# Issuing loads and stores from ScalarE's queue in a fused threshold-attention and MLP kernel

## The chip, the cores and the metric

The kernel runs on one core of one Trainium2 chip. The metric is the device time of one execution in microseconds (us). The core has TensorE (PE; its weight loads are shown apart as PEld), VectorE (DVE), ScalarE (ACT), GpSimd (POOL) and SyncE (SP). Each works through its own list of instructions in program order, and they wait for each other through semaphores. A DMA is started by an instruction in the list of one of these engines. "SPq" and "ACTq" in the profile are such issuing instructions on SyncE and ScalarE; the profile doesn't count them as busy time, but the queue they stand in is taken for as long as they last.

## The reference

All numbers are float32. `tau` is 0.02.

```python
# q, k, v: (8 batches, 8 heads, 576 rows, 64)
scores = 0.125 * (q @ k.T)                              # 576 x 576 for each head
scores = where(scores >= max(scores, axis=-1) - tau, scores, -1e9)
attn = exp(scores - max(scores, axis=-1))
attn = attn / (sum(attn, axis=-1) + 1e-9)
x = (attn @ v)                                          # regrouped: 4608 tokens x 512
h = maximum(x @ w_in, 0.0)                              # w_in: 512 x 2048
out = (h * h) @ w_out                                   # w_out: 2048 x 512, out: 4608 x 512
```

## The kernel before

**Work.** Attention is cut into *visits*. A visit is a pair of heads of one batch; there are 4 pairs per batch. The first batch is visited in two halves (visits 0 to 3 and 4 to 7), every other pair once (visits 8 to 35). A visit consists of *steps*: a step is a block of 128 query rows of both heads, and the last step of a full visit holds the remaining 64 rows of both. So a full visit has five steps.

A step does this. `scores` (L199) multiplies queries by keys into two PSUM tiles `s0`, `s1`, which exist once, and VectorE takes the row maxima (L204). `exponents` (L213, L215) runs on ScalarE. `threshold` (L227) on VectorE compares the scores with the threshold, multiplies and sums; after it the score tiles are free for the next step. `divide` (L237, L239) on GpSimd scales by the sum.

The attention weights must then be turned (keys onto partitions) for the product with the values, `mix` (L318). In the first visits PE turns them (L257) and ScalarE copies them out. From visit 11 on (`by_dma`) VectorE turns 32 x 32 blocks into the buffer `turned` (L288, two slots), and 48 DMAs per visit, 16 at a time, place the blocks in `wT` (L299, L306 in `place_blocks`). `mix` follows its step with a lag of four steps, and ScalarE copies its result into the ring `xT` (L332 to L347).

When 256 tokens are complete, the MLP for this *chunk* is put on a list of *pieces*: 16 pieces for the first product (L367, with ReLU on ScalarE, L377, and the square on GpSimd, L378), and then the second product. For chunks 0 and 1 that is `mlp_out` (L398); later ones use 14 pieces, `product` (L430), with sums and differences on VectorE (L441 to L457) that build the output rows `osb`.

**Order.** The program writes out the order for every engine by hand. One loop goes over the steps. In each step four calls of `fill(quarter)` take pieces from the list and put them between the parts of attention, so that PE always has MLP work beside attention. What follows a piece on other engines (`then`) is put down after the next piece, in `after`. The pieces left when attention is over run at the end.

**Loads and stores.** `load_qk(n)` (L161, L163) loads the query and key rows of visit `n` with 10 DMAs; `load_v(n)` (L171, L173) the values with 4. For full visits the rows of the next visit are loaded at the start of the second step, into one buffer each (`ql`, `kl`), which VectorE turns into `qT` and `kT` in `prep` (L178) at the end of the last step. The values go into two buffers in turn, and their loads are written at the end of the last step. `store_rows` (L411) stores 128 or 256 rows of output. All of these stand in SyncE's list, with the loads of the MLP weights (L122, early visits) and the placements: 1764 issues in all. Only visit 0's six key loads stand in ScalarE's.

Of the kernel before, what the change touches and what calls it, by code (L numbers as in the profile page):

```python
# [2 lines left out]

# [16 lines left out]
def kernel(  # L20
# [10 lines left out]
    nc = tc.nc  # L31
    B, H, S, D = q.shape
    d_model, d_ff = moe_w_in.shape
    n_tokens = out.shape[0]
    P = 128
    HP = H // 2
    NPAIR = B * HP
    NBLK = S // P
# [40 lines left out]
    at = RAW * 2 * WP  # L79
# [18 lines left out]
    osb = const.tile([P, 2, d_model], FP32, name="osb")  # L98
# [48 lines left out]
    def rows_of(n):  # L147
        return rows_in[n % 2 if n <= 2 * HP else 0]

    def load_qk(n):  # L150


        b, h = divmod(visits[n][0], HP)
        h *= 2
        for x, t in zip(rows_of(n), (q, k)):
            queue = nc.scalar if n == 0 and t is k else nc.sync
            for m in range(4):
                src = t[b, h + m // 2, :, (m % 2) * 32:(m % 2) * 32 + 32].rearrange("(c p) d -> p c d", p=32)
                last = REST // 32 if t is k and m >= 2 else 0
                to = x[m * 32:(m + 1) * 32, :, :]  # L160
                queue.dma_start(out=to[:, last:, :], in_=src[:, 0:S // 32 - last, :])  # L161
                if last:
                    queue.dma_start(out=to[:, 0:last, :], in_=src[:, S // 32 - last:, :])  # L163

    def load_v(n):
        b, h = divmod(visits[n][0], HP)
        h *= 2
        t = vs[n % 2]
        for u in range(2):
            at = u * (NBLK + 1)  # L170
            nc.sync.dma_start(out=t[:, at:at + NBLK, :],  # L171
                              in_=v[b, h + u, 0:NBLK * P, :].rearrange("(c p) d -> p c d", p=P))
            nc.sync.dma_start(out=t[u * D:(u + 1) * D, at + NBLK, :], in_=v[b, h + u, NBLK * P:S, :])  # L173

    def prep(n):

        for to, rows in zip((qT, kT), rows_of(n)):
            nc.vector.transpose(to, rows.rearrange("p c d -> p (c d)"))  # L178
        if NBLK in visits[n][1]:
            for u in range(2):  # L180
                rows = slice(u * D, (u + 1) * D)
                nc.gpsimd.tensor_copy(out=qmid[rows, u * D:(u + 1) * D], in_=qT[rows, NBLK * P:S])
# [127 lines left out]
    def mix(n, cols):  # L310
# [12 lines left out]
        def to(first, count):  # L323
            at = (lo + first) % RING
            assert at + count <= RING
            return xT[:, pr, at:at + count]
# [16 lines left out]
        else:  # L343
            fit = nq if whole else RING - lo % RING
            for x0, x1 in ((0, fit), (fit, nq)):
                if x0 < x1:
                    nc.scalar.copy(to(x0, x1 - x0), ps[:, x0:x1])  # L347

    ring3 = [6, 5, 7]
# [56 lines left out]

    def store_rows(j, t0, t1):
        lo = j * TCH  # L410
        nc.sync.dma_start(out=out[lo + t0 * P:lo + t1 * P, :].rearrange("(t p) d -> p t d", p=P), in_=osb[:, t0:t1, :])  # L411

# [2 lines left out]
    def product(j, x, half):  # L417

        if x == 0 and half == 0:
            a, c, b = ring3[2], ring3[0], ring3[1]  # L420
            used["abc"] = a, b, c
            ring3[:] = [b, a, c]
        a, b, c = (bank[y][:, 0:HD] for y in used["abc"])
        p = PRODUCTS[x]
        g0, g1 = g[:, 0:HF, :], g[:, HF:, :]
        left, slot, to = {
            "1": (g0[:, :, 0:P], Q00, a), "5": (gsum[0], FT1, c), "6": (gsum[1], FT2, b), "2": (g1[:, :, 0:P], Q10, a),
            "7": (gsum[0], FT3, b), "4": (g1[:, :, P:], FT4, a), "3": (gsum[1], Q11, c)}[p]
        for f in range(half * HF // 2, (half + 1) * HF // 2):
            nc.tensor.matmul(to, left[:, f, :], wo[:, slot, f, :], start=(f == 0), stop=(f == HF - 1))  # L430
        if not half:
            return []

        def halves(fn):
            for lo in (0, HF // 2):
                fn(slice(lo, lo + HF // 2))

        def then():
            add, sub, tt, u = ALU.add, ALU.subtract, nc.vector.tensor_tensor, u_sum
            if p == "1":  # L440
                nc.scalar.copy(p1s, a)  # L441
            elif p == "5":
                halves(lambda f: tt(out=gsum[0][:, f, :], in0=g0[:, f, 0:P], in1=g0[:, f, P:], op=sub))  # L443
            elif p == "6":
                tt(out=u, in0=b, in1=p1s, op=add)  # L445
                tt(out=osb[:, 0, HD:], in0=c, in1=u, op=add)
                halves(lambda f: tt(out=gsum[1][:, f, :], in0=g1[:, f, 0:P], in1=gsum[1][:, f, :], op=sub))
            elif p == "2":
                tt(out=osb[:, 0, 0:HD], in0=a, in1=p1s, op=add)  # L449
            elif p == "7":  # L450
                tt(out=u, in0=b, in1=u, op=add)
                tt(out=osb[:, 1, HD:], in0=c, in1=u, op=add)
            elif p == "4":
                tt(out=osb[:, 1, 0:HD], in0=u, in1=a, op=sub)
                store_rows(j, 1, 2)
            else:
                tt(out=osb[:, 0, HD:], in0=c, in1=osb[:, 0, HD:], op=add)  # L457
                store_rows(j, 0, 1)
        return [then]


# [32 lines left out]
    chunk_at, j = {}, 0  # L494
# [6 lines left out]
    state = {"us": 0.0, "left": 0.0, "step": 0, "rounded": 0, "then": []}  # L501
# [27 lines left out]
        return best  # L529

    def after():
        for fn in state["then"]:
            fn()
        state["then"] = []

    def fill(us):
        state["left"] += us
        while waiting and state["left"] >= PIECE_US / 2 and waiting[0][0] <= state["rounded"]:
            _, fn, *what = waiting.popleft()
            state["left"] -= PIECE_US  # L540
            if fn is mlp_out or what[0] <= PLAIN and what[1] == 0:
                after()
            then = fn(*what)
            after()
            state["then"] = then

# [26 lines left out]
    for s in range(END + 1):  # L573
        state["step"] = s
        on = s < NST
        now = []
        if on:
            n, i = steps[s]
            at = visits[n][1].index(i)
            last = at == len(visits[n][1]) - 1  # L580
            now = list(range(done, done + pieces[s]))
            done += pieces[s]
            more = n + 1 < len(visits)
            short = n < 2 * HP
            if short and at == 0 and 0 < n + 1 < 2 * HP:
                load_qk(n + 2)
            elif not short and at == 1 and more:
                load_qk(n + 1)
            if now:
                round_weights(now[0], 0)  # L590
            scores(s)
        old = steps[s - 2] if 2 <= s < NST + 2 and not by_dma(steps[s - 2][0]) else None
        at_once = now or old or early()
        lay = on and last and more and not by_dma(n)
        if old:
            turn(*old, 0)
            turn(*old, 1)
        if on:
            if at_once:
                exponents(n, i)  # L600
            if lay:
                prep(n + 1)
            elif now:
                round_weights(now[0], 1)
                round_weights(now[0], 2)
        if s in mixes and not old:
            mix(*mixes[s])
            for j in chunk_at.get(s, ()):
                add_chunk(j)
        if 0 < s <= NST and by_dma(steps[s - 1][0]):  # L610
            m, x = steps[s - 1]
            turn_blocks(m, x)
            if x % 2 or x == NBLK:
                place_blocks(m, x // 2)
        quarter = rate(s) / 4 if s < END else 1e9
        fill(quarter)
        if s in mixes and old:
            mix(*mixes[s])
            for j in chunk_at.get(s, ()):
                add_chunk(j)  # L620
        if old:
            turn(*old, 2)
        if on:
            if not at_once:
                exponents(n, i)
            threshold(n, i)
            if last and more and not lay:
                prep(n + 1)
            if lay and now:
                round_weights(now[0], 1)  # L630
                round_weights(now[0], 2)
        fill(quarter)
        if on:
            divide(n, i)
        fill(quarter)
        fill(quarter)
        if on:
            if now:
                end_rounding(now[0])
            for p in now[1:]:  # L640
                for stage in range(3):
                    round_weights(p, stage)
                end_rounding(p)
            if at == 0 and 0 < n <= 2 * HP:
                load_v(n)
            elif last and more and n >= 2 * HP:
                load_v(n + 1)
    after()
    assert not waiting


# [30 lines left out]
```

## Time and profile before

The median of three runs is 1451.44 us (1451.18 to 1452.18).

| what | value |
|---|---|
| profiled execution | 1450.02 us |
| its span, first to last instruction | 1448.2 us |
| mean granted TensorE clock | 0.992 |
| PE busy | 1387.1 us, 96% of the span |
| PE weight loads busy | 1058.0 us, 73% |
| VectorE busy | 904.5 us, 62% |
| GpSimd busy | 623.9 us, 43% |
| ScalarE busy | 423.1 us, 29% |
| DMA, mean of 16 engines, 300 to 1290 us | 0.51 |
| chain that ended last, share of the span | PE 65%, SPq 20%, DVE 6% |

The span is that of the slowest core, here the only one. Busy time is the time in which the engine executes instructions; the chain follows the last instruction back, at each step to what released it or to the instruction before it on its engine. Three parts can be told apart: the start and the visits that PE turns (to about 260 us, with the MLP weights being loaded and rounded beside them), the visits turned by DMA with MLP pieces between (about 260 to 1290 us), and the last chunks alone (about 1290 us to the end).

### The profile page before, as it was taken

The page shows a single profiled execution, that of the slowest core. Times are in us where ns is not written, and L with a number is a line of the kernel's source. Part 1 is how long each engine was busy: PE and PEld are TensorE (multiplying, and loading weights), DVE is VectorE, ACT ScalarE, POOL GpSimd, SP SyncE. Part 2 cuts the span into 40 slices and gives each one's busy share as a digit, 9 for nine tenths or more (in the row PEclk, how much of TensorE's full clock was granted, in tenths as well). Part 3 has the DMA queues.
Part 4 walks back from the last instruction along what each step waited for, and adds up shares of the span by engine and source line. Part 5 has one row for each costly group of instructions (what it writes and reads, how often), then busy time and mean ns, then how long its engine had stood idle before and what let it go on. Part 6 is the DMA issues. An engine that isn't in the chain of part 4 may idle for free.

```text
span 1448.2 us, 22131 instructions
## 1 busy us (share of the span) xinstructions
PE 1387.1 (96%) x7412; PEld 1058.0 (73%) x7412; DVE 904.5 (62%) x1930; ACT 423.1 (29%) x904; POOL 623.9 (43%) x794
## 2 busy tenths in 40 slices
PE   5898888999999999999999999999999999999998
PEld 3676555747787777777777777777777777788887
DVE  5899886568766676666675767666667666631011
ACT  3666554223222322222322222222222222210100
POOL 3588765425343444343343435343434352422321
PEclk9899999999999999999999999999999999999999
DMA  7564442345445545545455454555554445440000
GB/s 149 119 140 109 112 112 52 55 84 96 85 96 91 109 85 96 88 92 88 97 96 105 84 96 85 95 89 100 95 101 84 89 90 91 90 81 19 5 15 15
DMA packets 532528, 125.94 MB, mean 87 GB/s; under 512 B 523712, under 2 KB 523712, under 8 KB 532416
## 3 DMA queue, kind: packets, MB, share of 16 engines
q1 hardware_dynamic: 529984, 124.24, 44.7%
q8 instruction: 60, 0.98, 0.3%
q10 hardware_dynamic: 2400, 0.30, 0.2%
q14 instruction: 52, 0.43, 0.1%
q0 software_dynamic: 32, 0.00, 0.0%
HBM read 48.63 MB, written 9.44 MB: 40 GB/s over the span
## 4 chain that ended last, share of the span: by engine, by line
PE 65%; SPq 20%; DVE 6%; issue 3%; DMA 2%; ACT 2%; POOL 1%; DVEq 0%; ACTq 0%; POOLq 0%
PE bank L367 26%; PE bank L430 16%; SPq L299 12%; PE s L199 9%; PE bank L318 8%; SPq L306 5%; PE bank L398 3%; SPq L161 3%; DVE st L204 2%; PE bank L257 1%; SPq L163 1%; DVE w L227 1%; DVE turned L288 1%; DMA vs<-in_v_dram 1%; DVE turned L138 1%
## 5 line engine op out<-in xcount | busy, mean ns | idle before, releaser
L367 PE MATMUL bank<-xT,w_in_sb 128*128 128x256 f32 x2304 | 519.8, 382 | 3.5 <-POOL w_in_sb L144 2.4
L367 PEld LDWEIGHTS bank<-xT,w_in_sb 128*128 128x128 f32 x2304 | 431.6, 190 | 84.2 <-issue 21.3
L204 DVE TENSOR_REDUCE st<-s 128x1 f32<-128x576 f32 x288 | 206.7, 753 | 296.9 <-PE s L199 296.9
L378 POOL TENSOR_TENSOR g<-g 128x512 f32<-128x512 f32 x144 | 149.8, 1042 | 232.2 <-ACT g L377 209.4
L239 POOL TENSOR_SCALAR w<-w,st 128x576 f32<-128x576 f32 x269 | 236.4, 888 | 31.2 <-DVE st L230 25.2
L227 DVE SCALAR_TENSOR_TENSOR w<-s,st,w 128x576 f32<-128x576 f32 x269 | 207.3, 803 | 52.2 <-ACT w L215 51.9
L430 PE MATMUL bank<-wo,gsum 128*128 128x256 f32 x1024 | 234.2, 382 | 2.9 <-DVE u_sum L445 1.6
L430 PEld LDWEIGHTS bank<-wo,gsum 128*128 128x128 f32 x1024 | 192.5, 190 | 38.6 <-issue 7.6
L199 PE MATMUL s<-kT,qT 64*128 64x288 f32 x1024 | 176.8, 438 | 30.4 <-DVE kT L178 10.3
L237 POOL TENSOR_SCALAR st<-st 128x2 f32<-128x2 f32 (+1 forms) x160 | 38.7, 242 | 379.7 <-DVE w L227 366.1
L215 ACT ACTIVATE w<-s,st 128x576 f32<-128x576 f32 x269 | 186.1, 738 | 12.1 <-ACT st L213 0.4
L318 PE MATMUL bank<-wT,vs 128*64 128x128 f32 (+3 forms) x1700 | 179.7, 358 | 8.7 <-DMA wT<-turned 3.5
L430 PE MATMUL bank<-wo,g 128*128 128x256 f32 x768 | 178.7, 383 | 2.9 <-DVE osb L449 2.9
L199 PEld LDWEIGHTS s<-kT,qT 64*128 64x128 f32 x1024 | 101.1, 190 | 95.2 <-issue 71.4
L288 DVE STREAM_TRANSPOSE turned<-w 128x576 f32<-128x576 f32 x225 | 163.0, 758 | 10.1 <-DMA wT<-turned 3.8
L430 PEld LDWEIGHTS bank<-wo,g 128*128 128x128 f32 x768 | 143.8, 190 | 32.4 <-issue 8.2
L318 PEld LDWEIGHTS bank<-wT,vs 128*64 128x64 f32 x1700 | 107.9, 141 | 78.1 <-issue 25.6
L377 ACT ACTIVATE g<-bank 128x512 f32<-128x512 f32 x144 | 86.3, 599 | 200.7 <-PE bank L367 200.7
L213 ACT ACTIVATE st<-st 128x2 f32<-128x2 f32 (+1 forms) x160 | 33.2, 208 | 328.2 <-DVE st L204 327.5
L332 ACT COPY xT<-bank 128x256 f32<-128x256 f32 x42 | 15.7, 373 | 287.9 <-PE bank L318 287.9
L443 DVE TENSOR_TENSOR gsum<-g 128x512 f32<-128x512 f32 x32 | 20.8, 681 | 107.3 <-PE bank L430 107.3
L398 PE MATMUL bank<-wo,g 128*128 128x512 f32 x128 | 62.0, 619 | 7.3 <-POOL wo L144 7.0
(66 smaller groups left out, 858.1 us busy)
## 6 DMA issues: line engine op xcount, KB each, us to landing
wT<-turned SPq DMA_DIRECT2D x800, 72.0 KB, 2.2
ql<-in_q_dram SPq DMA_DIRECT2D x128, 72.0 KB, 2.5
vs<-in_v_dram SPq DMA_DIRECT2D x72, 128.0 KB, 2.5
wo<-in_moe_w_in_dram SPq DMA_DIRECT2D x16, 512.0 KB, 4.5
wo<-in_moe_w_out_dram SPq DMA_DIRECT2D x16, 512.0 KB, 3.6
out_dram<-osb SPq DMA_DIRECT2D x32, 256.0 KB, 2.3
kl<-in_k_dram SPq DMA_DIRECT2D x62, 72.0 KB, 2.6
wT<-turned SPq DMA_DIRECT2D x200, 20.0 KB, 1.9
```

The costliest lines, as they stand in the source:

```text
L199: nc.tensor.matmul(sc[u][:, half, 0:HALF], lhsT, kT[rows, half * HALF:(half + 1) * HALF], start=True, stop=True)
L204: nc.vector.tensor_reduce(out=mx[:, u:u + 1], in_=sc[u][:, :, 0:HALF], axis=AX.XY, op=ALU.max)
L215: nc.scalar.activation(out=w[:, u, :].rearrange("p (h k) -> p h k", h=2), in_=sc[u][:, :, 0:HALF], func=AF.Exp, bias=bias[:, u:u + 1], sca ...
L227: nc.vector.scalar_tensor_tensor(out=wu, in0=sc[u][:, :, 0:HALF], scalar=thr[:, u:u + 1], in1=wu, op0=ALU.is_ge, op1=ALU.mult, accum_out=s ...
L239: nc.gpsimd.tensor_scalar(out=w[:, u, :], in0=w[:, u, :], scalar1=z[:, u:u + 1], scalar2=rcp[:, u:u + 1], op0=ALU.add, op1=ALU.mult)
L288: nc.vector.transpose(wb[:, u * KB:(u + 1) * KB, i % 2, :], w[:, u, :].rearrange("p (k q) -> p k q", q=32))
L299: nc.sync.dma_start(out=to[:, :, at:at + 64], in_=wb[rows, j::4, :, :].rearrange("p c u q -> p c (u q)"))
L318: nc.tensor.matmul(ps[u * D:(u + 1) * D, 0:nq], vs[n % 2][:, u * (NBLK + 1) + c, :], wT[:, cw, cols], start=(c == 0), stop=(c == NBLK))
L367: nc.tensor.matmul(h[:, x % 2, :], w_in_sb[:, c, f * P:(f + 1) * P], xT[:, c, at:at + TCH], start=(c == 0), stop=(c == NMC - 1))
L378: nc.gpsimd.tensor_tensor(out=to, in0=to, in1=to, op=ALU.mult)
L398: nc.tensor.matmul(o[t].rearrange("p (h d) -> p h d", h=2), g[:, f, t * P:(t + 1) * P], mov, start=(f == 0), stop=(f == NFT - 1))
L430: nc.tensor.matmul(to, left[:, f, :], wo[:, slot, f, :], start=(f == 0), stop=(f == HF - 1))
```

## The change

Loads of visits after `2 * HP`, which is 8, are no longer issued where they are written. `load` puts them in a list, `loads`. `some_loads(count)` takes that many from its front and issues them, from ScalarE's queue. It is called for one after each MLP piece, and for one at four places in each step, between the quarters. If any are left before `prep` of the next visit in the steps turned by DMA, all are issued there. Loads of visits up to 8 stay as they were.

All stores are issued from ScalarE. Those of the chunks from 2 on are put at the front of the list (`later`) when the VectorE instruction that completes their rows is written, and so are issued at the next call. Those of chunks 0 and 1 are issued at once, after ScalarE's copies.

The placements and the weight loads stay on SyncE. No arithmetic changes.

```diff
+    loads = deque()
+
+    def some_loads(count):
+        for _ in range(min(count, len(loads))):
+            loads.popleft()()
+
+    def load(n, to, src):
+        if n <= 2 * HP:
+            nc.sync.dma_start(out=to, in_=src)
+        else:
+            loads.append(lambda: nc.scalar.dma_start(out=to, in_=src))
...
-            queue = nc.scalar if n == 0 and t is k else nc.sync
...
-                queue.dma_start(out=to[:, last:, :], in_=src[:, 0:S // 32 - last, :])
+                start = nc.scalar.dma_start if n == 0 and t is k else partial(load, n)
+                start(to[:, last:, :], src[:, 0:S // 32 - last, :])
                 if last:
-                    queue.dma_start(out=to[:, 0:last, :], in_=src[:, S // 32 - last:, :])
+                    start(to[:, 0:last, :], src[:, S // 32 - last:, :])
...
-            nc.sync.dma_start(out=t[:, at:at + NBLK, :],
-                              in_=v[b, h + u, 0:NBLK * P, :].rearrange("(c p) d -> p c d", p=P))
-            nc.sync.dma_start(out=t[u * D:(u + 1) * D, at + NBLK, :], in_=v[b, h + u, NBLK * P:S, :])
+            load(n, t[:, at:at + NBLK, :], v[b, h + u, 0:NBLK * P, :].rearrange("(c p) d -> p c d", p=P))
+            load(n, t[u * D:(u + 1) * D, at + NBLK, :], v[b, h + u, NBLK * P:S, :])
...
+    def later(fn):
+        loads.appendleft(fn)
...
-        nc.sync.dma_start(out=out[lo + t0 * P:lo + t1 * P, :].rearrange("(t p) d -> p t d", p=P), in_=osb[:, t0:t1, :])
+        nc.scalar.dma_start(out=out[lo + t0 * P:lo + t1 * P, :].rearrange("(t p) d -> p t d", p=P), in_=osb[:, t0:t1, :])
...
-                store_rows(j, 1, 2)
+                later(lambda: store_rows(j, 1, 2))
...
-                store_rows(j, 0, 1)
+                later(lambda: store_rows(j, 0, 1))
...
             then = fn(*what)
+            some_loads(1)
             after()
...
             threshold(n, i)
             if last and more and not lay:
+                some_loads(len(loads))
                 prep(n + 1)
...
+        some_loads(1)
         fill(quarter)
+        some_loads(1)
         if on:
             divide(n, i)
         fill(quarter)
+        some_loads(1)
         fill(quarter)
+        some_loads(1)
...
     after()
+    some_loads(len(loads))
```

More of the change, by code (lines that the diff above doesn't have):

```diff
@@ L2 @@
 from contextlib import ExitStack
+from functools import partial
 import concourse.bass as bass
@@ L531, in after @@
     def after():
-        for fn in state["then"]:
+        now, state["then"] = state["then"], []
+        for fn in now:
             fn()
-        state["then"] = []
     def fill(us):
```

## The prediction

> **What bounds the kernel now.** I first split the span into stages by busy time. Blocks of scores whose weights are turned by DMA fill about 262 to 1290 us; this is the stage that the change works on. Its middle, as busy time of each engine in one stretch (length, then PE, PE load, DVE, ACT, POOL, with instruction counts, then clock, DMA share and GB/s):
>
> ```profile
> 300.00:1290.00 990.00, 976.49 (x4984) 747.90 (x4983) 657.42 (x1415) 251.23 (x534) 402.31 (x535) 1.00 0.51 92
> ```
>
> TensorE is idle for only 990 - 976.5 = 13.5 us. Its queue order is fixed in the program, and after 1290 us it runs the remaining MLP work back to back (48.00 of 48.00 us in each of three windows). So a microsecond saved in the stage counts only if it is a microsecond of PE idle time, and the stage can give at most 13.5 us. ACT is busy for 251 of 990 us.
>
> The second view is SyncE's queue by order of time, one visit (a pair of heads) of the stage; columns are start, length, what, count:
>
> ```profile
> 603.99 22.46 SPq L299 DMA_DIRECT2D wT<-turned  x32
> 626.54 0.55 SPq L411 DMA_DIRECT2D out_dram<-osb  x1
> 627.13 0.44 SPq L171 DMA_DIRECT2D vs<-in_v_dram  x1
> ...
> 629.48 10.35 SPq L306 DMA_DIRECT2D wT<-turned  x16
> 639.92 0.54 SPq L411 DMA_DIRECT2D out_dram<-osb  x1
> ```
>
> One issue follows the other with no room between. Per visit there are 32 placements in 22.5 us and 16 in 10.35 us, 10 loads of queries and keys at about 0.53 us (5.3), 4 of values at about 0.58 (2.3), and 34 stores over about 27 visits, 1.3 at 0.55 (0.7): 41.2 us. A visit takes 5 steps of 8.3 us (mean distance between the first score matmuls of 123 steps), 41.5 us. SyncE's own waits from 300 to 1290 us add up to 19 us. **SyncE is full, like TensorE.**
>
> The third view asks whether the full queue makes PE wait: all waits of PE from 300 to 1290 us (total, times, longest).
>
> ```profile
> PE bank L318 <- DMA wT<-turned: 3.5, 4, 1.7
> PE bank L430 <- DVE osb L449: 2.9, 2, 1.9
> PE bank L430 <- DVE u_sum L445: 1.6, 1, 1.6
> PE s L199 <- DVE kT L178: 1.4, 3, 0.6
> PE bank L430 <- DVE osb L452: 1.2, 3, 0.5
> PE bank L367 <- ACT osb L405: 1.2, 1, 1.2
> PE bank L318 <- issue: 1.1, 2, 0.8
> PE s L199 <- DVE w L227: 0.5, 1, 0.5
> ```
>
> Only the first line is SyncE's: a mix (L318) stood before placements that landed late. Two more mixes waited 1.1 us with no releaser shown. The rest is the products (L430) waiting for VectorE, which stands behind its own thresholds in program order. The chain of waits gives SPq 20% of the span, but a chain names whoever came last, however short the wait; I go by the 13.5 us.
>
> **What the Trainium skill says.** "DMA: Bandwidth & Descriptors", section "Issuing engines are not separate DMA queues": DMAs of the scalar and sync engines run on the same 16 DMA engines, and a second issuer saves only sequencer time. The trace fits: transfers are busy for 0.51 of the stage, so sequencer time is the scarce thing. "Perfetto Trace Analysis", section "DMA Instruction — HWDGE (DVE, Sync)": the descriptor generator is shared and locked while one sequencer uses it. If that lock took most of an issue, ACT's issues would only queue behind SP's. The start of the trace speaks against it:
>
> ```profile
> 0.74 1.57 ACTq L161 DMA_DIRECT2D kl<-in_k_dram  x3
> 0.74 2.03 SPq L161 DMA_DIRECT2D ql<-in_q_dram  x4
> ```
>
> Seven issues run on two queues at once at 0.51 to 0.52 us each, as one queue alone does in the stage. The same title, "Identifying the Most-Contended Engine", warns that PE's busy share doesn't measure distance from its peak; I use it only as the bound on idle time.
>
> **The change, part by part.**
>
> *Loads leave SyncE.* By the code they do so from visit 9, the second pair of batch 1: 27 visits of 14 loads, 378. With 34 stores that is 412 issues. SyncE keeps 22.5 + 10.35 = 32.9 of 41.5 us per visit, 79%. It then waits for VectorE's transposes (L288) and placements go out at once. The mix stands about three steps (25 us) behind the program point of its placements; these need 16 x 0.66 + 2.2 to land = 12.8 us. So mixes stop waiting. Gain: 3.5 us, and half of the 1.1 whose cause isn't shown: 4.0. VectorE's waits for placements (L288, 3.5 us in 14 waits) go too; they lie on PE's path only in three product waits, 0.17 us each: 0.5. **Together -4.5 us.** Upper end 13.5, if all PE waits are echoes of SyncE; lower end 0, if PE runs into the next wait at once.
>
> *Loads enter ACT's queue.* An issue costs 0.5 us of ACT's sequencer (0.318 to 0.574 in the six at the start). 15.3 per visit add 8 us to 25% of 41.5 = 10.5: ACT is then taken for 45%. None of the loads should block: rows are free since the transposes before the visit's first scores, the values buffer since a mix more than a step ago. What is queued behind them: the exponents (L213, L215), for which VectorE's threshold (L227) waits, which frees the score banks for the next step's scores on PE. The room: between the last threshold of a step and the next step's scores lie, in the 49 steps with a mix, at least 1.5 us (median 2.35). There ACT is late already, behind the copy L332, and one more issue is absorbed. In the 73 without a mix the room is small: a tenth have 0.09 us or less, a quarter 0.53 or less, half 1.85. But there ACT is idle before the exponents:
>
> ```profile
> ACT st L213 <- DVE st L204: 299.4, 72, 7.8
> ```
>
> This is 4.2 us a time, and an issue without a wait runs in that idle time, as it stands earlier in the queue. The code pops one at a time; values come in the visit's first step (a mix step), queries and keys in its second and third. I charge one late issue in a tenth of the 73: 7 x 0.07 where room is left, up to 7 x 0.54: +0.5 us. If the cover fails, see the rivals. Squares (L377) are also behind loads; their bank comes round after three pairs of 3.45 us, so 0.
>
> *Before the stage.* Visits 9 to 11 have their loads issued from about 173 us on. From 173 to 262 ACT is busy 46 of 89 us, and some 40 issues put 21 us on top. PE there waits for POOL's weight pieces (L144, 7.0 us), which need ACT's first rounding step. The pops stand after the exponents, so what they delay is rounding and copies. Taken +0.6; bounds 0 and 15 steps x 0.54 = 8. SyncE's 21.1 us wait for the first store (L411 for ACT's osb), with visit 11's loads behind it, disappears; no engine waited for those loads: 0.
>
> *Stores.* A store waits on ACT for VectorE's osb. It is popped after a later piece, at the latest at the quarter's end, and the next step's exponents need a reduction that VectorE runs after that osb anyway; so it costs them its issue only, 25 x 0.4 in idle time: 0. In the tail ACT has nothing else. The last store follows L457 (1444.63, 0.42) by one issue on either queue: 0.
>
> Sum: -4.5 + 0.5 + 0.6 = -3.4 us. The profiled execution took 1450.0 us (span 1448.2, 1.8 around it), so 1446.6 with a span of 1444.8. The median before is 1451.4, which is 1.4 above the profiled one; carried over, **1448.0 us**.
>
> **Rivals.**
>
> *Hidden anyway.* The mix no longer waits, but PE then arrives earlier at products that wait for VectorE (5.7 us now) and stops there. For: half of the waits have nothing to do with SyncE. Against: mix waits and product waits are tens of us apart. Saves 1 us: 1450.4.
>
> *ACT becomes the late engine (slower).* Place: exponents of the second and third steps of a visit, 54 without a mix. If each comes 0.54 us late, a tenth lose 0.45 us and a further 15% about 0.25: 5.4 x 0.45 + 8.1 x 0.25 = 4.5 us; two issues in a row would cost 13. With 15 earlier steps at 0.54 = 8.1, less the gain: +8.1, 1459.5. It decides from the point where ACT's idle time before L213 is used up. For: ACT has no slack against a DMA that waits. Against: 4.2 us of idle a time.
>
> *All waits are SyncE's echo.* Saves 13.5: 1438. Against: in each product wait VectorE's queue shows thresholds ahead of osb, not transfers.
>
> *The change doesn't relieve.* Descriptor generation is one resource, the two queues share the 41 us: 1451.5. Against: the start of the trace.
>
> **How the numbers follow.** A measurement of this kernel tells some 0.2% (2.9 us) from no change. Chances: forecast 0.42 (of it 0.34 beyond 2.9 us, 0.08 within), hidden 0.22 (within), ACT late 0.23 (slower), all echo 0.08 (faster), no relief 0.05 (0.03 within, 0.02 slower). So faster 0.42, same 0.33, slower 0.25. The forecast's own range is 1444 to 1450. For 8 in 10: below, 1442.5 leaves out the echo; above, 1458 leaves out the worse half of the late ACT.
>
> **What would show it.** Right: SyncE waits for L288 by some 200 us in the stage, no PE wait for wT, issues on ACT of about 0.5 us, and L213 still waiting for L204. PE idle near 9 us from 300 to 1290. Wrong: new PE waits on L227 (scores) or on ACT's copies and squares, issues that grow to 0.8 us and more on both queues, or a longer stretch 173 to 262.

## The result, and where the time went

The changed kernel takes 1567.22 us (median of four runs, 1561.08 to 1567.86) against 1451.31 us before (four runs on the same chip, 1449.94 to 1452.18). The ratio is 1.079, with a 95% interval of 1.0762 to 1.0818: 7.9% slower, where 1448.0 us, a small gain, was forecast. The profiled execution took 1567.2 us with a span of 1565.4.

**Which stage.** The first block transposed for a placement and the last mix bound the stage in which weights are turned by DMA. The same stage, with the same 5443 matmuls, as one stretch in each kernel; columns as in the prediction (length, PE, PE load, DVE, ACT, POOL, clock, DMA share, GB/s). Before:

```profile
257.40:1340.40 1083.00, 1069.49 (x5443) 819.82 (x5441) 688.18 (x1482) 269.38 (x570) 431.75 (x570) 1.00 0.48 89
```

After:

```profile
259.50:1457.60 1198.10, 1119.75 (x5443) 845.93 (x5441) 683.48 (x1482) 271.25 (x570) 430.56 (x570) 0.96 0.44 80
```

The stage is 115.1 us longer; what lies ahead of it grew by 2.1 us, and what follows it takes 107.8 us in both. So 115.1 of the 117.2 us by which the span grew lie in this stage. TensorE's idle time there rose from 13.5 to 78.3 us (+64.8). Its busy time rose by 50.3 us for the same work, mostly because the granted clock fell: before, no stretch of the stage is at half clock; after, 17 stretches are, 85.3 us together, which at half speed cost 42.7 us. 64.8 + 42.7 = 107.5 of the 115.1 us; for the other 7.6 us, longer busy time, no cause is shown. ACT's own work is the same, 271.25 against 269.38 us: ACT did not become a busy engine.

**What TensorE waits for.** All its larger waits from 300 to 1290 us, changed kernel. The lines have moved by 12 to 15: scores are L211, thresholds L239, mixes L330, products L445, exponents L225 and L227.

```profile
PE s L211 <- DVE w L239: 29.5, 11, 5.6
PE bank L330 <- DMA wT<-turned: 16.3, 8, 4.0
PE bank L445 <- DVE osb L467: 11.9, 3, 6.1
PE bank L445 <- DVE u_sum L460: 4.0, 2, 2.4
PE bank L330 <- DMA out_dram<-osb: 3.2, 1, 3.2
```

The mix's wait for placements, which was to vanish, grew from 3.5 to 16.3 us, and scores now wait 29.5 us for thresholds, from 0.5.

**What the two issuing queues wait for.** SyncE, changed kernel, 300 to 1290 us:

```profile
SPq L311 <- DVE turned L300: 101.1, 23, 9.2
SPq L311 <- DMA vs<-in_v_dram: 75.2, 33, 5.8
SPq L318 <- DMA kl<-in_k_dram: 45.2, 12, 5.4
SPq L311 <- DMA out_dram<-osb: 28.6, 12, 6.2
SPq L318 <- DMA ql<-in_q_dram: 21.8, 4, 5.9
SPq L311 <- DMA ql<-in_q_dram: 20.8, 12, 4.0
```

The kernel before has this for the first of them, and no wait of SyncE for a DMA in that stretch:

```profile
SPq L299 <- DVE turned L288: 7.1, 4, 4.0
```

The first line is the relief that was forecast: SyncE runs dry and waits for VectorE's transposes. The other five are not. A placement copies transposed weights into wT; it neither reads nor writes the values, keys, queries or results. Yet placements wait for exactly those transfers, all now issued by ScalarE, 191.6 us in these lines. ScalarE in the same stretch (the idle time of the engine and what is shown as ending it):

```profile
ACT st L225 <- DVE st L216: 256.7, 59, 14.7
...
ACT st L225 <- DMA wT<-turned: 42.9, 6, 13.5
ACT g L392 <- DMA kl<-in_k_dram: 19.7, 8, 3.4
ACT g L392 <- DMA wT<-turned: 18.3, 5, 5.0
```

No exponent and no ReLU (L392) reads wT. In four of the five ReLU waits a load stands in front in ScalarE's queue that has itself waited for a placement. Of the six waits of the exponents, 42.9 us, this holds for two, 15.3 us. Counted at the loads and stores themselves, ScalarE's queue stands 71.8 us for placements, in 45 waits: 48.2 us at loads, 23.6 at stores.

**How that reaches the scores.** The prediction's path from a late queue to late scores led through ScalarE's exponents. The waits of VectorE in the same stretch show another, a transpose (L300) that waits for the placements to empty its slot of `turned`. Before and after:

```profile
DVE turned L288 <- DMA wT<-turned: 3.5, 14, 0.7
```

```profile
DVE turned L300 <- DMA wT<-turned: 48.6, 27, 6.9
```

The transpose stands ahead of the threshold in VectorE's order. From the chain of waits, 996 to 1008 us:

```profile
999.34 3.40 DMA ql<-in_q_dram
1002.74 0.02 issue
1002.75 2.16 DMA wT<-turned
...
1004.99 0.10 DVE turned L300
...
1006.43 0.72 DVE w L239 x2
1007.15 0.14 issue
1007.29 0.93 PE s L211 x2
```

A query load from ScalarE lands, SyncE can issue its placement, the transpose can start, then the threshold, and TensorE's scores after a stop of 3.77 us. Ten of the eleven waits of scores for thresholds, 28.3 of the 29.5 us, have such a held-up transpose just ahead of the threshold. The eleventh came through late exponents.

**One such wait, step by step.** The chain of waits of the changed kernel, 764 to 790 us (start, length, what):

```profile
770.86 2.32 DMA kl<-in_k_dram
773.18 0.02 issue
773.20 0.58 SPq L318
```

A key load, issued by ScalarE at 770.86, lands at 773.18, and 20 ns later a placement is issued on SyncE, which had stood still since 768.63. The built program says why. The program's builder gives each DMA of these two queues one of eight completion counters, in turn, and lets each DMA wait until the one before it on its counter has landed. These are the entries concerned, by position in the order in which counters are handed out, with the trace's issue times beside them:

```
position  queue    target        counter  issued   the one before on this counter
   878    SyncE    wT   (L311)      6     765.35   870 SyncE   wT
   879    ScalarE  kl   (L161)      7     770.86   871 SyncE   wT
   886    SyncE    wT   (L318)      6     768.04   878 SyncE   wT
   887    SyncE    wT   (L318)      7     773.20   879 ScalarE kl   <- waits 4.6 us
   894    SyncE    wT   (L318)      6     778.68   886 SyncE   wT
   902    ScalarE  kl   (L161)      6     780.57   894 SyncE   wT   <- waits 3.3 us
   904    ScalarE  kl   (L161)      0     781.88   896 SyncE   wT
```

Position 887 could not go before 879 had landed, which comes ahead of it in the handed-out order, but sat in ScalarE's queue behind exponents. Then the debt is returned: ScalarE's load 902 is free to go when the last exponent ends at 777.22, but waits for placement 894, which is late because 887 was. What that did to ScalarE's queue and to TensorE (timeline; in brackets the idle time before, and what ended it):

```profile
770.86 2.25 ACTq L161 DMA_DIRECT2D kl<-in_k_dram  x4
...
780.57 1.63 ACTq L161 DMA_DIRECT2D kl<-in_k_dram  x2
782.24 0.60 ACT L392 ACTIVATE g<-bank 128x512 f32<-128x512 f32 x1 [5.03 <-DMA wT<-turned]
```

```profile
785.40 4.57 PE L330 MATMUL bank<-wT,vs 128*64 128x320 f32 x18 [3.97 <-DMA wT<-turned]
```

The ReLU on ScalarE starts after 5.03 us of idle time, and TensorE stops for 3.97 us before the mix: the sixteen placements had taken 15.75 us instead of 10.35, and the last, issued at 783.20, landed at 785.05. The clock of TensorE around that stop, as two stretches:

```profile
780.00:785.80 5.80, 1.83 (x14) 0.77 (x12) 2.80 (x5) 0.60 (x1) 2.72 (x4) 1.00 0.31 50
785.80:789.20 3.40, 3.40 (x16) 1.79 (x13) 0.29 (x1) 0.00 (x0) 0.00 (x0) 0.50 0.63 112
```

After the stop the matmuls run at 0.50 for 3.4 us. So a stop of 4 us costs nearly 6.

The other waits are of the same kind. The five lines above and a shorter one of the same sort (4.3 us) are 74 waits of SyncE. In 68 of them, 178.3 us, the placement was issued within 0.15 us of the landing of the DMA eight positions before it, a DMA of ScalarE. The other six stand at a separate instruction that waits for a key load.

**Why the kernel before doesn't have it.** It has the same eight counters. But there SyncE issues nearly everything: the eighth DMA back is eight issues of 0.65 us, 5.2 us, in the past, and a placement lands in 2.2 us. So that wait is over when its turn comes, and from 300 to 1290 us the trace shows none. Counted in the built programs, DMAs whose predecessor on the counter is on the other queue: 4 in the kernel before (all where the first keys are loaded), 518 in the changed one (258 of SyncE that wait for ScalarE, 260 the other way). The Trainium skill ("DMA: Bandwidth & Descriptors", section "Why a DMA increments its semaphore by 16 and not by 1") gives a reason for such a wait: with two DMAs in flight on one semaphore its count doesn't tell which of them has landed. No run here shows that; the runs show what the wait costs.

### The profile page after: what moved, and what is told of

It reads as the page before. It is cut to its first block, busy times and chain, and to the rows that moved or that the text cites. A ratio compares the mean times of both kernels' runs of the same rounds, so it can differ in the third digit from the quotient of the medians.

```text
span 1565.4 us, 22062 instructions
## 1 busy us (share of the span) xinstructions
PE 1441.8 (92%) x7412; PEld 1087.9 (69%) x7412; DVE 898.6 (57%) x1930; ACT 425.3 (27%) x904; POOL 622.4 (40%) x794
## 4 chain that ended last, share of the span: by engine, by line
PE 70%; DVE 8%; DMA 8%; SPq 8%; ACT 3%; issue 2%; POOL 1%; ACTq 1%; DVEq 0%; POOLq 0%
PE bank L382 25%; PE bank L445 19%; PE s L211 11%; PE bank L330 11%; SPq L318 6%; PE bank L413 3%; DMA wT<-turned 3%; DVE st L216 2%; DMA ql<-in_q_dram 2%; DMA kl<-in_k_dram 2%; SPq L311 1%; PE bank L269 1%; DVE w L239 1%; DVE turned L300 1%; ACT w L227 1%
## 5 line engine op out<-in xcount | busy, mean ns | idle before, releaser
L382 PE MATMUL bank<-xT,w_in_sb 128*128 128x256 f32 x2304 | 528.9, 387 | 2.1 <-ACT osb L420 1.1
L382 PEld LDWEIGHTS bank<-xT,w_in_sb 128*128 128x128 f32 x2304 | 438.9, 193 | 86.4 <-issue 22.7
L239 DVE SCALAR_TENSOR_TENSOR w<-s,st,w 128x576 f32<-128x576 f32 x269 | 207.5, 804 | 98.2 <-ACT w L227 97.9
L445 PE MATMUL bank<-wo,gsum 128*128 128x256 f32 x1024 | 238.1, 386 | 17.2 <-DVE osb L467 11.9
L211 PE MATMUL s<-kT,qT 64*128 64x288 f32 x1024 | 195.3, 457 | 62.6 <-DVE w L239 44.7
L445 PEld LDWEIGHTS bank<-wo,gsum 128*128 128x128 f32 x1024 | 195.2, 193 | 54.3 <-DVE osb L467 13.4
L330 PE MATMUL bank<-wT,vs 128*64 128x128 f32 (+3 forms) x1700 | 198.4, 375 | 27.0 <-DMA wT<-turned 19.9
L300 DVE STREAM_TRANSPOSE turned<-w 128x576 f32<-128x576 f32 x225 | 163.0, 758 | 79.7 <-DMA wT<-turned 53.9
L211 PEld LDWEIGHTS s<-kT,qT 64*128 64x128 f32 x1024 | 109.1, 198 | 134.2 <-issue 109.4
L330 PEld LDWEIGHTS bank<-wT,vs 128*64 128x64 f32 x1700 | 115.5, 146 | 107.0 <-issue 56.6
L227 ACT ACTIVATE w<-s,st 128x576 f32<-128x576 f32 x269 | 185.9, 737 | 12.4 <-ACT st L225 0.7
L445 PE MATMUL bank<-wo,g 128*128 128x256 f32 x768 | 181.5, 387 | 1.9 <-DVE osb L464 1.9
L445 PEld LDWEIGHTS bank<-wo,g 128*128 128x128 f32 x768 | 145.9, 193 | 32.4 <-issue 9.6
L392 ACT ACTIVATE g<-bank 128x512 f32<-128x512 f32 x144 | 86.1, 599 | 255.5 <-PE bank L382 184.2
L225 ACT ACTIVATE st<-st 128x2 f32<-128x2 f32 (+1 forms) x160 | 33.1, 207 | 366.4 <-DVE st L216 308.5
```

Of the source, the lines that this page charges most:

```text
L211: nc.tensor.matmul(sc[u][:, half, 0:HALF], lhsT, kT[rows, half * HALF:(half + 1) * HALF], start=True, stop=True)
L227: nc.scalar.activation(out=w[:, u, :].rearrange("p (h k) -> p h k", h=2), in_=sc[u][:, :, 0:HALF], func=AF.Exp, bias=bias[:, u:u + 1], sca ...
L239: nc.vector.scalar_tensor_tensor(out=wu, in0=sc[u][:, :, 0:HALF], scalar=thr[:, u:u + 1], in1=wu, op0=ALU.is_ge, op1=ALU.mult, accum_out=s ...
L300: nc.vector.transpose(wb[:, u * KB:(u + 1) * KB, i % 2, :], w[:, u, :].rearrange("p (k q) -> p k q", q=32))
L330: nc.tensor.matmul(ps[u * D:(u + 1) * D, 0:nq], vs[n % 2][:, u * (NBLK + 1) + c, :], wT[:, cw, cols], start=(c == 0), stop=(c == NBLK))
L382: nc.tensor.matmul(h[:, x % 2, :], w_in_sb[:, c, f * P:(f + 1) * P], xT[:, c, at:at + TCH], start=(c == 0), stop=(c == NMC - 1))
```

## The experiments

The theory: the loss comes from completion counters that two hardware queues share. The rivals: loads come later than before, and somebody waits for them; ScalarE has less room than the prediction found; the stores alone do it; or putting loads one by one between other work does it. The diffs are against the changed kernel and cut where "..." stands. "Before" is the kernel before on the same chip.

**e1, the same late places, but SyncE's queue.** Nothing but the queue goes back.

```diff
-            loads.append(lambda: nc.scalar.dma_start(out=to, in_=src))
+            loads.append(lambda: nc.sync.dma_start(out=to, in_=src))
...
-        nc.scalar.dma_start(out=out[lo + t0 * P:...
+        nc.sync.dma_start(out=out[lo + t0 * P:...
```

> The changed kernel with its loads and stores issued at the same late places, one at a time, but from SyncE. Shared counters (each hardware DMA takes the next of eight completion counters, whichever queue it stands in, and waits until the DMA before it on that counter has landed, so two queues hold each other up): one queue again, so the loss is gone, 1445 to 1460 us. ScalarE's time (the issues keep ScalarE from its exponents): also gone, 1445 to 1460. Late loads (what hurts is that loads and stores come later and one at a time): the loss stays, above 1540.

Measured 1459.37 us against 1454.23, ratio 1.0037 (1.0023 to 1.005). Loading late has a price, and a line that shows it (waits of VectorE, 300 to 1290 us):

```profile
DVE kT L190 <- DMA kl<-in_k_dram: 16.7, 11, 3.4
```

The kernel before has no such line. But it is 5 us of 116. Lateness falls as the main cause.

**e2, the same late places, GpSimd's queue.**

```diff
-            loads.append(lambda: nc.scalar.dma_start(out=to, in_=src))
+            loads.append(lambda: nc.gpsimd.dma_start(out=to, in_=src))
...
-        nc.scalar.dma_start(out=out[lo + t0 * P:...
+        nc.gpsimd.dma_start(out=out[lo + t0 * P:...
```

In the built program GpSimd's DMAs have counters of their own; of the DMAs of SyncE and ScalarE only the 4 at the start still depend on the other queue.

> The same loads and stores, issued at the same places from GpSimd, whose software DMAs have counters of their own. Shared counters: SyncE keeps its relief and is no longer held up by other queues' loads; GpSimd pays about 0.8 us for each of some 412 issues (the one in the trace of before took 0.77), 43% busy becomes 60%; 1445 to 1475 us, and no wait of SyncE for the landing of a load. ScalarE's time: also 1445 to 1475. Competition of transfers (two queues' packets slow each other): the loss stays, above 1530.

Measured 1467.66, ratio 1.0087 (1.0063 to 1.0111). The stage itself is faster than before: 1080.0 us, from 1083.0, with 11.3 us of TensorE idle, and SyncE's waits are as forecast for the change:

```profile
SPq L311 <- DVE turned L300: 210.0, 48, 6.9
```

No wait for a load is left in SyncE's list. The loss lies before the stage, which begins at 275.0 instead of 257.4: there GpSimd has weights to prepare, and loads of 0.67 us each are put between them (e10 leaves these on SyncE). So a second queue with separate counters relieves SyncE without the waits.

**e3, ScalarE busier without DMAs.** Loads and stores back on SyncE, the loads at their old places; two copies of 128 x 128 are added on ScalarE at each place where the change issues a DMA late.

```diff
+    def work():
+        for _ in range(2):
+            nc.scalar.copy(scrap, ident)
...
-            loads.append(lambda: nc.scalar.dma_start(out=to, in_=src))
+            nc.sync.dma_start(out=to, in_=src)
+            loads.append(work)
...
```

> Loads and stores on SyncE as before; at every place where the changed kernel issues from ScalarE, ScalarE instead copies a 128x128 tile twice, about 0.55 us of work without any wait. The output is the same; the copies go to a tile that nobody reads. Shared counters: only ScalarE's time is lost, 1450 to 1465 us. ScalarE's time: the loss comes back, 1530 or more.

Measured 1456.53, ratio 1.0017 (1.0005 to 1.0029). From 300 to 1290 us:

```profile
300.00:1290.00 990.00, 974.72 (x4957) 744.75 (x4956) 653.88 (x1417) 440.13 (x1231) 402.52 (x537) 1.00 0.50 92
```

ScalarE works 440 us instead of 251, and TensorE idles 15.3 us instead of 13.5. ScalarE's time is not the cause; the prediction's reading of its idle room was right.

**e4, tiny DMAs on ScalarE.** As e3, but at each place ScalarE issues one DMA of 128 x 4 bytes into a scratch tile that nobody reads.

```diff
+    def work():
+        x = count["tiny"] % 64
+        count["tiny"] += 1
+        nc.scalar.dma_start(out=scrap[:, x:x + 1], in_=tau.to_broadcast([P, 1]))
...
```

> Loads and stores on SyncE as before; at every place where the changed kernel issues from ScalarE, it issues a DMA of 128 x 4 bytes into a tile that nobody reads. SyncE is not relieved, nothing waits for the tiny DMAs' data. Shared counters: the tiny DMAs take their turn in the eight counters and couple the queues, so the loss appears without any load being moved: 1530 us or more, with SyncE's placements waiting for the tiny DMAs to land. ScalarE's time: as in the run with copies, since an issue takes about as long. Competition or lateness of loads: no loss, about 1450 to 1465.

Measured 1780.18, ratio 1.2235 (1.2206 to 1.2264). SyncE's waits, 300 to 1290 us:

```profile
SPq L319 <- DMA scrap<-in_tau_dram: 207.7, 88, 7.2
SPq L319 <- DMA wT<-turned: 33.6, 24, 3.5
```

Placements wait for transfers with which they share no data at all, 88 times. What they share is the counter: 568 DMAs depend on the other queue. Nothing was taken off SyncE here. TensorE idles 271 us in the stage, and 341 us of the whole run are at half clock. (e12 asks for the DMAs' own share of this.)

**e5, loads where they should not interleave.** Loads on ScalarE in groups, in steps in which SyncE was thought to issue no placements between; stores back on SyncE.

```diff
+            v_next = not short and at == 3 and more
...
+        if on and v_next:
+            load_v(n + 1)
...
-            elif last and more and n >= 2 * HP:
-                load_v(n + 1)
+            if at == 1 and n >= 2 * HP:
+                some_loads(len(loads))
+            if at == 3 and more and n >= 2 * HP:
+                some_loads(len(loads))
```

> Loads on ScalarE as in the changed kernel, but moved to other places in the program: those of queries and keys all within the visit's second step (what is left is issued at its end), those of values in its fourth step instead of the next visit's first; stores on SyncE. So the eight DMAs written before any load are placements that were written at least half a step earlier, and the eight written before any placement are loads that ScalarE reaches well before the placements are due. Shared counters: the coupling stays but the DMA waited for has landed already; most of the loss is gone, 1445 to 1480 us. ScalarE's time: as many issues and more of them in a row, the loss stays, 1530 or more.

Measured 1594.81, ratio 1.0973 (1.095 to 1.0995): a miss. In the built program 518 DMAs still depend on the other queue (261 and 257), and queries and keys alternate with placements one by one. The counters follow the order in which the builder plans the issues of all queues, not the order in which they are written. In time they drift apart again (waits of SyncE, 300 to 1290 us):

```profile
SPq L311 <- DMA ql<-in_q_dram: 69.0, 17, 8.8
SPq L311 <- DMA vs<-in_v_dram: 57.2, 26, 5.2
```

The theory of the counters stands; that the written order controls them is gone.

**e6, only the loads on ScalarE, and e7, only the stores.** In e6 `store_rows` uses `nc.sync` and isn't put off; in e7 the loads are issued with `nc.sync` at their old places.

```diff
e6:
-        nc.scalar.dma_start(out=out[lo + t0 * P:...
+        nc.sync.dma_start(out=out[lo + t0 * P:...
...
-                later(lambda: store_rows(j, 1, 2))
+                store_rows(j, 1, 2)
...
e7:
-            loads.append(lambda: nc.scalar.dma_start(out=to, in_=src))
+            nc.sync.dma_start(out=to, in_=src)
```

> Only the loads go to ScalarE, one at a time as in the changed kernel; stores stay on SyncE. Shared counters: 378 of 412 couplings stay, and a store on SyncE that waits for VectorE now also holds counters; 1530 to 1580 us. Stores that wait for VectorE in ScalarE's queue as the main cause: most of the loss gone, below 1490.

> Only the stores go to ScalarE; loads stay on SyncE as before. Shared counters: 24 couplings in the stage; each store is waited for by the eighth DMA after it on SyncE, which is full, and waits itself for SyncE's backlog; 1455 to 1490 us. Stores waiting for VectorE as the main cause: most of the loss is here, above 1530.

e6: 1559.83 against 1452.63, ratio 1.0741 (1.0717 to 1.0766), with 474 DMAs that depend on the other queue. e7: 1486.92, ratio 1.0234 (1.0214 to 1.0255), with 64. So 34 stores cost 34 us by themselves, a microsecond each. SyncE in e7:

```profile
SPq L311 <- DMA out_dram<-osb: 49.4, 15, 8.1
```

Each store waits on ScalarE for VectorE's result, and a placement whose counter it has waits with it. The two parts add up to 141 us, more than the 116 of both, so they don't simply add; neither is the sole cause.

**e8, the loads of every second visit.**

```diff
-        if n <= 2 * HP:
+        if n <= 2 * HP or n % 2 == 0:
```

(with the stores on SyncE, as in e6.)

> As the run with only the loads on ScalarE, but for every second visit; the loads of the others stay on SyncE at their old places. In the built program 149 placements or other SyncE DMAs and 145 of ScalarE's wait for a counter last used by the other queue, where the run with all loads has 239 and 235. Shared counters: the loss follows the count of such waits, about 0.6 of 107 us, 1500 to 1530 us. A loss that comes from a single bad place or from the start: not in proportion, near 1452 or near 1560.

Measured 1542.54 against 1451.74, ratio 1.0627 (1.0606 to 1.0649). Dependent DMAs fell from 474 to 294, 0.62 of e6; the loss only from 107 to 91 us, 0.85. The size was missed. SyncE's waits for loads from 300 to 1290 us did follow the count, 126.4 us from 199.0 in e6. That SyncE is relieved half as much and so has less room to catch up is argued, not shown.

**e9, loads on ScalarE at their old places.** As e6, but ten and four in a row.

```diff
-            loads.append(lambda: nc.scalar.dma_start(out=to, in_=src))
+            nc.scalar.dma_start(out=to, in_=src)
```

> Loads on ScalarE at the places where they were written before, ten and four in a row, not one at a time; stores on SyncE. 261 and 257 waits on the other queue's counters. Shared counters: about the loss of the run with all loads, 1540 to 1610 us. Spreading the loads out as the cause: the loss is gone, below 1480.

Measured 1554.28, ratio 1.072 (1.069 to 1.075), with 518 dependent DMAs. Spreading the loads over other work, the change's care for ScalarE, neither causes the loss nor saves from it.

**e10, loads from GpSimd, after the start.** What e2 lost at the start is left on SyncE: from visit 12 on the loads go one at a time from GpSimd, all others and the stores from SyncE.

```diff
-        if n <= 2 * HP:
+        if n < 3 * HP:
...
-            loads.append(lambda: nc.scalar.dma_start(out=to, in_=src))
+            loads.append(lambda: nc.gpsimd.dma_start(out=to, in_=src))
...
```

> Loads of visits from 12 on from GpSimd, one at a time; the earlier ones, and all stores, on SyncE. This keeps GpSimd's issues out of the stage before 260 us, in which PE waits for GpSimd's weight pieces. Relief of SyncE without coupling, the part of the forecast that the changed kernel couldn't show: SyncE gets free time, PE's waits for placements vanish, 3 to 5 us faster than before, 1446 to 1450. Relief worth nothing: the time of before within 1 us, or slower by what GpSimd's issues cost.

Measured **1447.82** (ten runs) against 1451.74, ratio 0.9974 (0.9965 to 0.9983): faster than both kernels. The same stretch and waits as before:

```profile
300.00:1290.00 990.00, 979.63 (x4994) 747.26 (x4995) 662.86 (x1420) 252.58 (x537) 606.82 (x857) 1.00 0.47 93
```

```profile
SPq L311 <- DVE turned L300: 194.1, 47, 6.9
```

TensorE idles 10.4 us, no wait of it for wT is left, SyncE waits 194 us for transposes, and the stage takes 1079.0 us, 4.0 less than before. This is what the prediction had worked out for ScalarE, here with the loads of 24 visits of its 27 and without the stores.

**e11, the same at the old places.** Ten and four in a row, as the kernel before has them on SyncE. Against e10:

```diff
-            loads.append(lambda: nc.gpsimd.dma_start(out=to, in_=src))
+            nc.gpsimd.dma_start(out=to, in_=src)
```

> The same loads from GpSimd, but at the places where they were written before, ten and four in a row (about 8 us of GpSimd's queue at a time). Relief as in the run beside it; GpSimd's divisions come late behind ten issues, so some of it is lost: 1447 to 1458.

Measured 1455.3, ratio 1.0029 (1.0017 to 1.004); the stage takes 1087.3 us, 8.3 more than e10. On GpSimd the places matter, where on ScalarE they didn't. That ten issues in a row hold up GpSimd's own work, which thresholds and mixes need in time, is argued, not shown.

**e12, the tiny DMAs of e4 from GpSimd.** Against e4:

```diff
-        nc.scalar.dma_start(out=scrap[:, x:x + 1], in_=tau.to_broadcast([P, 1]))
+        nc.gpsimd.dma_start(out=scrap[:, x:x + 1], in_=tau.to_broadcast([P, 1]))
```

> The tiny DMAs of the other run at the same places, issued from GpSimd, whose counters no SyncE or ScalarE DMA uses; all loads and stores stay on SyncE. Shared counters: no coupling, so only what GpSimd's issues cost, as in the run with all loads on GpSimd, 1455 to 1480 us. If the tiny transfers themselves, or a second stream of transfers, had cost the 330 us: above 1600.

Measured 1544.61 against 1454.95, ratio 1.063 (1.0601 to 1.066): a miss. SyncE waits for none of them any more, as expected. But transfers land later: the median of query loads is 5.4 us instead of 2.5, of the 20 KB placements 3.4 instead of 1.9. TensorE then waits at the mixes:

```profile
PE bank L338 <- issue: 17.5, 8, 4.7
PE bank L338 <- DMA ql<-in_q_dram: 12.8, 6, 4.9
```

The query loads also take longer to issue, 0.84 us on the mean instead of 0.54, and 13 of the 90 us lie ahead of the stage, which begins at 270.2. So at most some 90 of the 326 us of e4 can be due to the tiny DMAs themselves, if the cost carries over, and about 236 are left for the counters. It does not carry over as it is: in e4 query loads land in 2.7 us and the 20 KB placements in 1.9; of the large loads only the values come clearly later (3.8 us, before 2.5). Why DMAs of half a kilobyte from GpSimd delay the others so much stays open. In the changed kernel this plays no part: its placements land in 2.2 and 1.9 us, its query loads in 2.5, as before.

**What was not tried.** Loads on ScalarE with counters of their own: the builder hands them out, and no way for the kernel to choose them was tried. So the one direct comparison is missing. GpSimd's DMAs may differ in more than the counters (e12), so e2 and e10 alone would not settle it. The theory rests on the same loads with shared counters (the changed kernel, e6, e9) and with separate ones (e2, e10), on transfers without any shared data (e4), and on the waits above, matched with the counters of the program.

## Why the prediction was wrong

**The step that failed** is in "Loads enter ACT's queue": "None of the loads should block: rows are free since the transposes before the visit's first scores, the values buffer since a mix more than a step ago." The buffers are free, as it says: in the built program none of the 378 loads has a wait for TensorE, VectorE or GpSimd. The loads block nevertheless, on the DMA that had their counter before. The step asked only which data a DMA depends on. In its place the runs showed 191.6 us of SyncE's waits for ScalarE's transfers, 71.8 us of ScalarE's for SyncE's, and a stage that is 115.1 us longer.

**"Loads leave SyncE", -4.5 us**: right as a mechanism and in size, where nothing takes it back. e10 has it, with -3.9 us in the median and -4.0 in the stage, the mix waits gone and 194 us of SyncE waiting for transposes where about 200 were forecast. In the changed kernel that wait is only 101 us, and the waits of VectorE's transposes for placements, which were to go, rose from 3.5 to 48.6 us.

**"Loads enter ACT's queue", +0.5 us for issue time**: close for what it counted. Issues on ScalarE take 0.42 to 0.52 us on the mean for loads and 0.38 for stores; e3 adds 189 us of work there for 2 us. The cover that was named, ScalarE's idle time before the exponents, covers time that ScalarE spends, not a wait whose end lies with another queue. The 0 for what it calls squares (L377 is the ReLU; the square is GpSimd's) fails with it: that wait for placements is 18.3 us.

**"Before the stage", +0.6**: measured +2.1, inside the bounds of 0 and 8. **The tail**: 107.8 us in both, as forecast.

**"Stores", 0**: wrong, for the same reason as the loads. The step looked at who is queued behind a store on ScalarE; e7 shows who waits for it on SyncE: 34 us for 34 stores.

**The rivals.** "Hidden anyway" and "all waits are SyncE's echo" aren't what happened. "The change doesn't relieve", by a shared descriptor generator: no issue became longer (placements 0.63 us on the mean in both kernels). "ACT becomes the late engine" had the sign and even the sentence, "ACT has no slack against a DMA that waits", and the scores do wait for thresholds. But its place was the exponents, where the trace shows VectorE's transposes, and it priced late issues at 8 us, not waits. Of the signs listed for a failure the first appeared, scores that wait; issues didn't grow, and the most telling sign, a placement that waits for a load, was not on the list.

**What the trace before could have told.** Not the size of the loss, but that there is such a wait. In the first 7 us keys are loaded from ScalarE and queries from SyncE, and SyncE's waits over the whole span of the kernel before have this line:

```profile
SPq L161 <- DMA kl<-in_k_dram: 1.3, 1, 1.3
```

A load of the next visit's query rows stands on SyncE from 4.88 to 6.17 us, until a key load of ScalarE lands at 6.16. It reads and writes nothing of that key load; in the built program it has its counter. The prediction took its evidence for two queues from the seven issues just ahead of this one.

## What to carry to other kernels

Before moving DMAs to a second queue, ask not only whether their buffers are free, but which completion counters they share with the first queue: each queue may stand still until the other's transfer lands, in an order fixed when the program is built. Here the relief came from an engine whose DMAs have separate counters (GpSimd, from the point where it has room: 1447.82 us, a gain of 0.3%). And a wait between two transfers that share no data is the sign of it in a profile: look at the waits of the DMA queues for tiles that the line doesn't touch.

## What was not expected of the hardware

- **Half-clock stretches follow short stops.** 17 stretches of 3.4 to 10.2 us at 0.50 lie in the stage of the changed kernel and none in that of the kernel before; they cost 42.7 us, two thirds of what the stops themselves cost. Each begins during a stop of TensorE of over 1 us or within 2.4 us of its end. The Trainium skill ("TensorE: Matmul & The Clock Gate", section "HAM oscillation — how this bites in real kernels") asks for no idle gaps over about 3.4 us. The lengths of the stretches agree with that window; the gaps don't need to be so long here: in the 12 us ahead of the stretch at 731.19 the only gap over 0.7 us is one of 1.3 us, and ahead of that at 833.59 one of 1.9. Nine of the stage's 26 stops of over 1 us have no stretch, one of them 3.3 us long.
- **One microsecond per store.** 34 stores on a second queue cost 34 us, though each takes 0.4 us to issue and lands in 2.2.
- **Tiny DMAs from GpSimd delay large ones.** With 410 transfers of 0.5 KB from GpSimd, query loads landed in 5.4 us instead of 2.5, and the run was 90 us slower (e12). From ScalarE the same transfers left query loads at 2.7 us (e4). The cause is open.
